# Selecting v over all rows of TensorE, and the last dilated queries in natural order

## The chip, the cores and the metric

The kernel runs on one core of one Trainium2 chip. The metric is the device time of one execution in microseconds (us), the median of several runs; lower is better. A core has five engines: TensorE (PE; its weight loads are shown apart as PEld), VectorE (DVE), ScalarE (ACT), GpSimd (POOL) and SyncE (SP). Matmuls write PSUM, which has eight banks; everything else lives in SBUF. Transfers run on 16 DMA engines. Here POOL issues the loads, which convert float32 to float16 on the way, and SP issues the stores.

## The reference

Attention over 8 batches, 8 heads, 576 positions and 64 features, with two kinds of window, followed by a soft mixture of 8 experts with 4 slots each:

```python
scores = scale * np.matmul(q, k.transpose(0, 1, 3, 2))
rel = pos[:, None] - pos[None, :]
mask_plain = (rel >= 0) & (rel < 32)
mask_dil = (rel >= 0) & (rel < 32 * 4) & (rel % 4 == 0)
masks = np.stack([mask_plain if h < 4 else mask_dil for h in range(8)])
x = softmax(np.where(masks, scores, -1e9)) @ v        # then (B*S, H*D) = (4608, 512)

logits = x @ phi                                      # phi: (512, 32)
d = softmax over the 4608 rows of logits
slot_input = d.T @ x                                  # 32 slots
slot_out[e] = relu(slot_input[e] @ w1[e]) @ w2[e]     # w1: (512, 1024), w2: (1024, 512)
c = softmax over the 32 columns of logits
out = c @ slot_out                                    # (4608, 512), float32
```

The softmax over all 4608 rows means that no expert can start before the last batch's attention is done, and that no row of the output can be written before the last expert.

## The kernel before

**Loads.** `load_batch` (L154) brings q, k and v of one batch into one of eight "home" tiles, with `DMA_DIRECT2D` issues on POOL. When a batch has been read out of its home, `load_w1` and `load_w2` (L236, L245) put an expert's weights there. POOL's order is written by hand (L599 puts POOL under a manual schedule): all eight batches, then w1 and w2 of experts 0 to 5, w1 of 6, w1 of 7, w2 of 6, and w2 of 7 in two halves. A load into a home waits for the home's last readers. The order of the other engines' instructions is the planner's, so the lines of one step may be spread between those of others.

**Attention** goes in 32 units of two heads of a batch, in the order plain, dilated, plain, dilated (L255). A unit's steps run staggered (L611 to L646): `transposes` of q and k, `scores`, `softmax_parts` (exponential on ACT, product with a mask on DVE), `values` (probabilities times v, with a column of ones in v that gives the denominators, then the division on DVE), and `x_transposes`. Per batch come `front_logits`, `front_rows` and `front_slots` for the logits, their exponentials by rows and the sum of slots. Queries and keys are taken in blocks of 128; the last block holds queries 512 to 575.

In the dilated units position 4t + c belongs to class c. Blocks 0 to 3 of the output are the first 128 queries of each class; block 4 has the last 16 of each class. Before, query t of class c stands in partition 32c + t of block 4, 16 used and 16 idle partitions a class. So block 4 takes 16 matmuls with 32 columns of weights each (L391 to L394: 4 classes, and two sources of v: rows of class c, and the last 64 positions), the copy into xT reorders it (L426), `front_rows` needs four extra narrow matmuls (`row_blocks`, L449), and the masks of the two parts are built once by `spread_masks` (L564).

**v for plain units and for the tails.** v arrives with four positions in one partition. `spread_v` (L193) copies the dilated one. `select_v` (L198) turns the plain one into blocks of 128 positions by matmuls with 0/1 matrices (`pick`): for each block, four matmuls over 32 partitions, which use 32 rows of TensorE at one of two row positions; two blocks go into one tile of the score banks (`ps_s`, tag "s") and ACT copies them out (L213). A third tile in the ring takes the last 64 positions: four matmuls over 16 partitions for the plain heads (L216), four with 32 columns for the dilated ones (L225), and one copy (L234).

**PSUM.** `ring` has two banks and serves, in turn, every transposed q, k and x, the logits, the rows, the sums of slots and the third tile of `select_v`; a new use waits until the one two before it has been copied out. `ps_s` has two tiles of two banks (scores; and two tiles of `select_v` a batch), `ps_o` two of one bank (values).

**The end.** `last_early`, `last_logits` and `last_slots` finish the last batch; `expert_in` and `expert_out` run the experts as the weights land, `sop` (L699) sums them, `so` is its copy (L716), and the output phase (L726 to L749) multiplies, scales on ACT and DVE, and stores on SP's queue.

Of the kernel before, what the change touches and what calls it, by code (L numbers as in the profile page):

```python
# [35 lines left out]
CL = S // DIL  # L36
DW = CL + 16
# [6 lines left out]
def constants():  # L44
    j = np.arange(128)[:, None]
    i = np.arange(QW)[None, :]
    d = i - j
    keep = ((d >= 0) & (d < WINDOW)).astype(np.float16)
    m, n = np.arange(128)[:, None], np.arange(64)[None, :]
    ends = (m // 32 == n // 16) & (m % 32 <= n % 16)  # L50
    band = np.concatenate([keep, ends], axis=1).astype(np.float16)
    ident = np.eye(128, dtype=np.float16)
    return band, ident
# [3 lines left out]
def kernel(  # L57
# [17 lines left out]
    mask = consts.tile([128, QW + 2 * N_SLOTS + 256], FP16, name="mask")  # L75
# [7 lines left out]
    nc.sync.dma_start(out=mask[:, 0 : QW + 64], in_=band_dram.ap())  # L83
# [14 lines left out]
    pick = kept([128, 4, 32, 4], "pick")  # L98
    stackI = kept([128, N_SLOTS], "stackI", FP32)
    upper = kept([128, 1], "upper", FP32)  # L100
    phi_by = kept([128, 4, 4, N_SLOTS], "phi_by")
# [10 lines left out]
    nc.vector.memset(phi_by, 0.0)  # L112
# [3 lines left out]
    P2 = kept([128, 2, 4, 2, 32], "P2")  # L116
# [4 lines left out]
    Er = [kept([128, 10, N_SLOTS], f"Er{i}") for i in range(2)]  # L121
# [6 lines left out]
    nc.vector.memset(P2, 0.0)  # L128
    nc.vector.memset(P2[0:1, :, :, 0, 16:32], 1.0)
# [68 lines left out]
    def select_v(b):  # L198
        raw, last = raws[b]["vp"], raws[b]["vt"]
        for i in range(2):  # L200
            sel = ps_s.tile([128, 2, 2, 4, D], FP32, name=f"sel{b}_{i}", tag="s")
            for r in range(4):
                for n in range(2):
                    rows = slice(64 * i + 32 * n, 64 * i + 32 * n + 32)
                    nc.tensor.matmul(  # L205
                        sel[:, n, 0],
                        pick[rows, r].rearrange("p i j -> p (i j)"),
                        raw[rows, :, r, :],
                        start=(r == 0),
                        stop=(r == 3),  # L210
                        tile_position=(64 * i + 32 * n, 0),
                    )
            nc.scalar.copy(out=vp[b % NV][:, 2 * i : 2 * i + 2, :, 0:D], in_=sel[:, :, 0])  # L213
        end = ring.tile([128, 2, 4, D], FP32, name=f"sel{b}_2", tag="ring")
        for r in range(4):
            nc.tensor.matmul(  # L216
                end[:, 0],
                pick[96:112, r].rearrange("p i j -> p (i j)"),
                last[:, 0:4, r, :],
# [3 lines left out]
            )  # L223
        for r in range(4):
            nc.tensor.matmul(  # L225
                end[32 * r : 32 * r + 32, 1],
                ident[96:112, 96:128],
                last[:, 4:8, r, :],
                start=True,
                stop=True,  # L230
                tile_position=(96, 32 * r),
                skip_group_check=True,
            )
# [66 lines left out]
    def scores(u):  # L300
# [3 lines left out]
        for part in range(2):  # L304
# [7 lines left out]
            for at, k0, q0, n in todo:  # L312
                for g in range(2):
                    ks = q0 - 32 * g - 64 * (at // DW) if k0 is None else k0
# [10 lines left out]
    def softmax_parts(u, tiles):  # L325
# [24 lines left out]
        if hp < 2:  # L350
# [8 lines left out]

        nc.vector.tensor_tensor(  # L360
            out=P2.rearrange("p a c s t -> p (a c) s t")[:, :, :, 0:16],
            in0=pr[:, :, :, 128:DW].rearrange("p a c (s t) -> p (a c) s t", s=2),
            in1=mask[:, QW + 64 :].rearrange("p (c s t) -> p c s t", c=8, s=2),
# [3 lines left out]
    def values(u):  # L367
# [7 lines left out]
        for half in range(2):  # L375
# [4 lines left out]
            for i, blk in enumerate(blocks):  # L380
                for h in range(2):
# [7 lines left out]
                    else:  # L389
                        for s in range(2):  # L390
                            for c in range(4):  # L391
                                vt = vp[b % NV][:, 5, hl + h] if s else vd[b % 2][:, 4 * (hl + h) + c]
                                mms.append((ot[32 * c : 32 * c + 32, i, h], P2[:, h, c, s], vt))
# [15 lines left out]
    def x_transposes(u):  # L409
# [11 lines left out]
        else:  # L421
# [4 lines left out]
            nc.vector.tensor_copy(  # L426
                out=xT[:, hp, 512:576].rearrange("c (t k) -> c t k", k=4),
                in_=rg[:, 512:640].rearrange("c (k t) -> c t k", k=4)[:, 0:16],
            )

# [19 lines left out]
    row_blocks = [(slice(0, 128), 128 * i, 1) for i in range(4)]  # L450
    row_blocks += [(slice(0, 128), c, 4) for c in range(4)] + [(slice(0, 128), 512, 1)]
    row_blocks += [(slice(32 * c, 32 * c + 32), 512 + c, 4) for c in range(4)]

    def rows(to, tokens, rhs, start, stop):
        for n, (part, at, step) in enumerate(row_blocks):
            w = step * (part.stop - part.start - 1) + 1
            nc.tensor.matmul(
                to[part, min(n, 9), :], tokens(at, at + w, step), rhs, start=start, stop=stop,
# [3 lines left out]
    def front_rows(b):  # L462
# [7 lines left out]
        ep = ring.tile([128, 11, N_SLOTS], FP32, name=f"e{b}", tag="ring")  # L470
        if b < B - 1:
            rows(ep, lambda a, z, s: ET[:, r0 + a : r0 + z : s], ident[:, 0:N_SLOTS], True, True)
            nc.vector.tensor_copy(out=Er[b % 2], in_=ep[:, 0:10])
        for n, (_, c0, nj) in enumerate(cols):
            nc.tensor.matmul(
                ep[:, 10, n : n + 1], ET[:, c0 : c0 + 127 * nj + 1 : nj], quarter, start=True, stop=True
            )
        if cols:
            n0 = cols[0][0]
            nc.vector.reciprocal(out=rrow[:, n0 : n0 + len(cols)], in_=ep[:, 10, 0 : len(cols)])  # L480

    def front_slots(b):
# [4 lines left out]
        for n, (g, blk, j) in enumerate(order):  # L487
            e_col = 8 + g if blk == 4 else 4 * g + blk
# [14 lines left out]
    def last_early(last):  # L503
# [4 lines left out]
        for dc in range(4):  # L508
# [8 lines left out]
        lr = last[:, 1, 0 : 11 * N_SLOTS].rearrange("p (i s) -> p i s", s=N_SLOTS)  # L517
        nc.tensor.matmul(
            lr[:, 8:10].rearrange("p i s -> p (i s)"), ident, mask[:, QW : QW + 64],
# [261 lines left out]
```

## Time and profile before

| | |
|---|---|
| three runs | 184.94, 185.99 and 186.16 us; median 185.99 |
| span of the profiled execution, first to last instruction | 183.5 us (the page has no other figure for it) |
| median of the runs less that span | 2.5 us |
| matmuls | 2595, with as many weight loads |
| loads by POOL's queue | 30.79 MB in SBUF; 93.9% of 16 engines' span |
| stores by SP's queue, with a few small loads | 9.89 MB; 13.4% |
| HBM read and written | 62.02 and 9.44 MB |
| select, L205 | 128 matmuls, 17.8 us busy, 307 ns from start to end of one |
| its two copies a batch, L213 | 16, 9.4 us busy, 590 ns |
| third tile: L216, L225, copy L234 | 5.6, 2.5 and 4.7 us busy |
| narrow values of L395 (32 columns) | 256 matmuls, 4.8 + 4.6 us busy |
| product for block 4, L360 | 16, 4.5 us busy, 282 ns |
| reorder of block 4, L426 | 16, 3.5 us busy, 221 ns |

Matmuls are pipelined: one takes 200 to 300 ns from start to end, while the next may start 30 to 110 ns after it. What PE pays is therefore read from the starts in the timeline, not from the mean length. The line of 40 slices shows busy tenths of equal parts of the span (9 is 90% or more). A chain of work is read downwards in order of time: start, length, and what ran or what was waited for; the step after a DMA is what that DMA released. In a row of waits come the waiting instruction, what released it, the sum in us, the number of waits and the longest.

### The profile page before, as it was taken

How to read it: one execution, taken by the hardware profiler on the slowest of the kernel's cores; microseconds unless marked ns; L12 is line 12 of the kernel's file. 1: busy time of each engine (PE TensorE's matmuls, PEld its weight loads, DVE VectorE, ACT ScalarE, POOL GpSimd, SP SyncE). 2: the span in 40 equal slices, each digit the busy share in tenths (PEclk: the TensorE clock that was granted, in tenths of full speed). 3: DMA queues.
4: the chain of work that ended last, by engine and by line, in shares of the span. 5: the costliest groups of instructions: out<-in, count | busy, mean ns of one | idle time of the engine just before them, and what ended most of it. 6: DMA issues, size and time to landing. Idle time of an engine off the chain costs nothing.

```text
span 183.5 us, 6054 instructions
## 1 busy us (share of the span) xinstructions
PE 151.8 (83%) x2595; PEld 105.8 (58%) x2595; DVE 117.1 (64%) x363; ACT 115.5 (63%) x208; POOL 46.9 (26%) x77
## 2 busy tenths in 40 slices
PE   1869999999988989998997998898979998885300
PEld 1637776677676667666765767666768644432000
DVE  7605886388877877878779687786970111496410
ACT  2248845689599789779878959977703022675410
POOL 7752555464554654401102001003100000000000
PEclk9999999999999999999999999999995589998555
DMA  5999999999999999999999999999999995199996
GB/s 103 183 203 203 202 203 201 202 202 204 204 201 201 204 199 204 226 211 221 212 216 216 212 216 216 218 212 218 218 214 220 212 208 105 75 440 427 427 427 262
DMA packets 23978, 41.06 MB, mean 224 GB/s; under 512 B 1680, under 2 KB 20240, under 8 KB 21136
## 3 DMA queue, kind: packets, MB, share of 16 engines
q0 software_dynamic: 21584, 30.79, 93.9%
q1 hardware_dynamic: 2368, 9.89, 13.4%
q8 instruction: 20, 0.33, 0.6%
q14 instruction: 6, 0.05, 0.1%
HBM read 62.02 MB, written 9.44 MB: 389 GB/s over the span
## 4 chain that ended last, share of the span: by engine, by line
DMA 74%; issue 15%; POOL 3%; ACT 2%; DVE 1%; PE 0%; POOLq 0%; DVEq 0%; SPq 0%
DMA home<-in_moe_w_dram 31%; DMA home<-in_v_dram 15%; DMA home<-in_k_dram 12%; DMA home<-in_q_dram 9%; DMA out_dram<-ot 7%; ACT ot L739 2%; DVE ot L741 1%; POOL home L250 1%; POOL home L162 1%; POOL home L239 1%; POOL home L184 0%; POOL home L187 0%; ACT so L716 0%; PE sop L699 0%; PE f L735 0%
## 5 line engine op out<-in xcount | busy, mean ns | idle before, releaser
L400 DVE TENSOR_TENSOR x<-o,rc 128x384 f16<-128x384 f32 x64 | 29.9, 482 | 0.5
L332 ACT ACTIVATE pr<-s 128x960 f16<-128x960 f32 (+1 forms) x32 | 24.7, 780 | 1.8 <-PE s L315 1.8
L344 ACT ACTIVATE pd<-s 128x640 f16<-128x640 f32 x32 | 20.9, 706 | 1.7 <-PE s L315 1.7
L162 POOL DMA_DIRECT2D home<-in_v_dram x24 | 16.6, 692 | 16.6 <-DMA home<-in_k_dram 11.6
L205 PE MATMUL sel<-home,pick 32*128 32x256 f16 x128 | 17.8, 307 | 1.4 <-DMA home<-in_v_dram 1.1
L399 DVE RECIPROCAL rc<-o 128x6 f32<-128x6 f32 x64 | 10.2, 177 | 13.5 <-PE o L395 13.4
L416 PE MATMUL rgx<-ident,x 128*128 128x128 f16 x160 | 15.6, 233 | 3.0 <-ACT qT L295 3.0
L741 DVE TENSOR_SCALAR ot<-f,rrow 128x512 f32<-128x512 f32 (+1 forms) x19 | 12.5, 716 | 7.7 <-DMA out_dram<-ot 5.2
L335 DVE TENSOR_TENSOR Pp<-pr,mask 128x960 f16<-128x960 f16 (+2 forms) x48 | 16.4, 394 | 0.4 <-ACT pr L332 0.4
L280 ACT COPY qT<-rgq 128x576 f16<-128x576 f16 x16 | 10.3, 641 | 9.0 <-PE rgq L275 8.5
L422 ACT COPY xT<-rgx 128x512 f16<-128x512 f16 x16 | 9.6, 601 | 10.0 <-PE rgx L416 10.0
L739 ACT ACTIVATE ot<-f,rrow 128x512 f32<-128x512 f32 (+1 forms) x19 | 11.2, 675 | 7.0 <-DMA out_dram<-ot 6.6
L239 POOL DMA_DIRECT2D home<-in_moe_w_dram x8 | 4.3, 534 | 44.4 <-PE rgq L290 36.5
L213 ACT CAST vp<-sel 128x512 f16<-128x512 f32 x16 | 9.4, 590 | 9.2 <-PE sel L205 9.0
L416 PEld LDWEIGHTS <-x 128*128 128x128 f16 x160 | 10.2, 102 | 7.2 <-issue 5.4
L735 PE MATMUL f<-so,ET 128*128 128x512 f16 (+1 forms) x38 | 11.0, 402 | 3.9 <-ACT ot L739 3.0
L275 PEld LDWEIGHTS <-home 96*64 96x64 f16 x384 | 11.9, 123 | 3.9 <-issue 2.0
L184 POOL DMA_DIRECT2D home<-in_k_dram x16 | 10.6, 661 | 10.1 <-DMA home<-in_q_dram 8.2
L395 PE MATMUL o<-vp,Pp 128*128 128x65 f16 x288 | 12.9, 203 | 0.0
L436 PE MATMUL l<-xT,phi 128*128 128x288 f16 x64 | 10.8, 304 | 2.0 <-ACT qT L280 1.7
L295 DVE COPY kTd<-rgk 128x576 f16<-128x576 f16 x16 | 12.0, 752 | 0.6 <-PE rgk L290 0.5
L295 ACT COPY qT<-rgq 128x576 f16<-128x576 f16 x16 | 10.3, 646 | 3.1 <-PE rgq L290 2.6
(105 smaller groups left out, 292.9 us busy)
## 6 DMA issues: line engine op xcount, KB each, us to landing
home<-in_moe_w_dram POOLq DMA_DIRECT2D x15, 1024.0 KB, 30.1
out_dram<-ot SPq DMA_DIRECT2D x7, 1024.0 KB, 7.5
home<-in_k_dram POOLq DMA_DIRECT2D x16, 288.0 KB, 9.9
home<-in_q_dram POOLq DMA_DIRECT2D x15, 288.0 KB, 9.7
home<-in_v_dram POOLq DMA_DIRECT2D x16, 256.0 KB, 9.8
out_dram<-ot SPq DMA_DIRECT2D x3, 512.0 KB, 6.5
home<-in_moe_w_dram POOLq DMA_DIRECT2D x2, 512.0 KB, 27.3
home<-in_v_dram POOLq DMA_DIRECT2D x8, 64.0 KB, 8.9
```

What stands on the lines that cost most here:

```text
L162: nc.gpsimd.dma_start(out=dst, in_=v[b, h0 : h0 + n_h, r0 : r0 + 4 * n_p, :].rearrange("h (p r) d -> p h (r d)", r=4),)
L205: nc.tensor.matmul(sel[:, n, 0], pick[rows, r].rearrange("p i j -> p (i j)"), raw[rows, :, r, :], start=(r == 0), stop=(r == 3), tile_posi ...
L275: nc.tensor.transpose(rg[64 * h : 64 * h + 64, r, :], raw[:, 2 * hp + h, D * r : D * r + D], ident[0:NP, 0:NP],)
L295: (nc.scalar.copy if nm == "q" else nc.vector.tensor_copy)(out=dst[:, 0:S].rearrange("c (g p a) -> c g p a", g=4, a=3), in_=rg.rearrange(" ...
L332: nc.scalar.activation(out=pr, in_=st[:, :, 0:n], func=AF.Exp, scale=SCALE)
L335: nc.vector.tensor_tensor(out=Pp[:, :, b0 : b0 + nb, 0:w], in0=pr[:, :, at : at + nb * w].rearrange("p h (t c) -> p h t c", c=w), in1=mask ...
L344: nc.scalar.activation(out=pr[:, part].rearrange("p c e t -> p e c t"), in_=st[:, :, 0 : 2 * DW].rearrange("p e (c t) -> p e c t", c=2), f ...
L395: nc.tensor.matmul(to, lhs, rhs, start=(n == 0), stop=(n == len(mms) - 1), skip_group_check=True)
L400: nc.vector.tensor_tensor(out=x[:, blocks[0] : blocks[0] + nb, D * hl : D * hl + 2 * D].rearrange("p t (h d) -> p t h d", h=2), in0=ot[:, ...
L416: nc.tensor.transpose(rg[:, 128 * blk : 128 * blk + 128], x[:, blk, hl : hl + 128], ident)
L739: nc.scalar.activation(out=ot[:, j, d0:d1], in_=fp, func=AF.Copy, scale=scale)
L741: nc.vector.tensor_scalar(out=ot[:, j, d0:d1], in0=fp, scalar1=scale, scalar2=None, op0=ALU.mult)
```

## The change

- `select_v`: for each block of 128 positions four matmuls now run over all 128 partitions, with `pick` as a zero-padded matrix from which a shifted window of 128 columns is cut. Its two tiles are in the ring, not in the score banks. The third tile takes all eight heads at once: four matmuls of 512 columns over 16 partitions with a second matrix, `pick_end`.
- Block 4 of the dilated units is kept in natural order: query 4t + c in partition 4t + c. Its probabilities go into `Pm` (four matmuls a head with 128 columns of weights, one per class) and `Pt` (one matmul a head for the last 64 positions): 10 matmuls a unit in place of 16. The product on DVE becomes two.
- `front_rows` and the rows of the last batch have 9 matmuls in place of 13; `Er` has 9 blocks, not 10. The copy of block 4 into xT no longer reorders, and takes 64 columns as they stand.
- Setup: `spread_masks` goes, `spread_ends` builds `pick_end`, the mask of the tails comes from the constant `band` (same size), `shut` is a small tile of its own, and `spread_phi` casts phi once and uses 16 matmuls of 32 columns in place of 4 of 128.

No transfer is added, moved or resized, and POOL's order is the same. Core of the diff:

```diff
-    P2 = kept([128, 2, 4, 2, 32], "P2")
+    Pm = kept([128, 2, 4 * 129], "Pm")
+    Pt = kept([128, 2, 128], "Pt")
...
     def select_v(b):
         raw, last = raws[b]["vp"], raws[b]["vt"]
         for i in range(2):
-            sel = ps_s.tile([128, 2, 2, 4, D], FP32, name=f"sel{b}_{i}", tag="s")
-            for r in range(4):
-                for n in range(2):
-                    rows = slice(64 * i + 32 * n, 64 * i + 32 * n + 32)
+            sel = ring.tile([128, 2, 4, D], FP32, name=f"sel{b}_{i}", tag="ring")
+            for n in range(2):
+                for r in range(4):
                     nc.tensor.matmul(
-                        sel[:, n, 0],
-                        pick[rows, r].rearrange("p i j -> p (i j)"),
-                        raw[rows, :, r, :],
+                        sel[:, n],
+                        pick[:, 2 * i + n, 3 - r : 131 - r],
+                        raw[:, :, r, :],
                         start=(r == 0),
                         stop=(r == 3),
-                        tile_position=(64 * i + 32 * n, 0),
                     )
-            nc.scalar.copy(out=vp[b % NV][:, 2 * i : 2 * i + 2, :, 0:D], in_=sel[:, :, 0])
-        end = ring.tile([128, 2, 4, D], FP32, name=f"sel{b}_2", tag="ring")
+            nc.scalar.copy(out=vp[b % NV][:, 2 * i : 2 * i + 2, :, 0:D], in_=sel)
+        end = ring.tile([128, 2, 4, D], FP32, name=f"end{b}", tag="ring")
         for r in range(4):
             nc.tensor.matmul(
-                end[:, 0],
-                pick[96:112, r].rearrange("p i j -> p (i j)"),
-                last[:, 0:4, r, :],
+                end.rearrange("p a h d -> p (a h) d"),
+                pick_end[96:112, 128 * r : 128 * r + 128],
+                last[:, :, r, :],
                 start=(r == 0),
                 stop=(r == 3),
                 tile_position=(96, 0),
-            )
-        for r in range(4):
-            nc.tensor.matmul(
-                end[32 * r : 32 * r + 32, 1],
-                ident[96:112, 96:128],
-                last[:, 4:8, r, :],
...
+        tails = pr[:, :, :, 128:DW].rearrange("p a c (s t) -> p a c s t", s=2)
         nc.vector.tensor_tensor(
-            out=P2.rearrange("p a c s t -> p (a c) s t")[:, :, :, 0:16],
-            in0=pr[:, :, :, 128:DW].rearrange("p a c (s t) -> p (a c) s t", s=2),
-            in1=mask[:, QW + 64 :].rearrange("p (c s t) -> p c s t", c=8, s=2),
+            out=Pm.rearrange("p a (c x) -> p (a c) x", c=4)[:, :, 0 : 4 * TAIL : 4],
+            in0=tails[:, :, :, 0].rearrange("p a c t -> p (a c) t"),
+            in1=mask[:, None, 128:CL].broadcast_to([128, 8, TAIL]),
+            op=ALU.mult,
+        )
+        nc.vector.tensor_tensor(
+            out=Pt[:, :, 0 : 4 * TAIL].rearrange("p a (t c) -> p a c t", c=4),
+            in0=tails[:, :, :, 1],
+            in1=ends[:, None].broadcast_to([128, 2, 4, TAIL]),
             op=ALU.mult,
         )
...
-                        for s in range(2):
-                            for c in range(4):
-                                vt = vp[b % NV][:, 5, hl + h] if s else vd[b % 2][:, 4 * (hl + h) + c]
-                                mms.append((ot[32 * c : 32 * c + 32, i, h], P2[:, h, c, s], vt))
+                        for c in range(4):
+                            mms.append((ot[:, i, h], Pm[:, h, 128 * c : 128 * c + 128], vd[b % 2][:, 4 * (hl + h) + c]))
+                        mms.append((ot[:, i, h], Pt[:, h], vp[b % NV][:, 5, hl + h]))
...
-            nc.vector.tensor_copy(
-                out=xT[:, hp, 512:576].rearrange("c (t k) -> c t k", k=4),
-                in_=rg[:, 512:640].rearrange("c (k t) -> c t k", k=4)[:, 0:16],
-            )
-
+            nc.vector.tensor_copy(out=xT[:, hp, 512:576], in_=rg[:, 512:576])
...
-    row_blocks = [(slice(0, 128), 128 * i, 1) for i in range(4)]
-    row_blocks += [(slice(0, 128), c, 4) for c in range(4)] + [(slice(0, 128), 512, 1)]
-    row_blocks += [(slice(32 * c, 32 * c + 32), 512 + c, 4) for c in range(4)]
+    row_blocks = [(128 * i, 1) for i in range(4)] + [(c, 4) for c in range(4)] + [(512, 1)]
...
-        for r in range(4):
-            nc.tensor.matmul(
-                pp,
-                pick[:, r].rearrange("p i j -> p (i j)"),
-                phi_by[:, :, r, :],
+            for r in range(4):
+                nc.tensor.matmul(
+                    pp[:, kc], pick[:, kc, 3 - r : 131 - r], phi_h[:, r, :],
```

## The prediction

> **What bounds the kernel now.** I read the page first: queues and the row of 40 slices, then the chain, then the seam where the weights end, and only then PE, where the change is.
>
> ```profile
> span 183.5 us, 6054 instructions
> PE 151.8 (83%) x2595; PEld 105.8 (58%) x2595; DVE 117.1 (64%) x363; ACT 115.5 (63%) x208; POOL 46.9 (26%) x77
> DMA  5999999999999999999999999999999995199996
> q0 software_dynamic: 21584, 30.79, 93.9%
> q8 instruction: 20, 0.33, 0.6%
> ```
>
> PE is the busiest compute engine, but the DMA engines are full in every slice except the first and two near the end: 30.79 MB of loads on POOL's queue, then the stores. The chain in order of time says who released whom at that gap:
>
> ```profile
> 128.48 28.27 DMA home<-in_moe_w_dram
> 156.74 0.04 issue
> 156.78 0.42 PE sop L699 x4
> 157.21 0.02 issue
> 157.23 0.59 ACT so L716
> ```
>
> The last half of w2 of expert 7 is issued at 128.48 and lands at 156.74; four sop matmuls, the copy and the output phase follow. POOL was held before that issue: its waits have "home L239 <- PE rgq L290" with 36.5 us in 3 waits (home 7 must be read out), the last ending at 126.91. That is no starvation: behind that point only w1 of 7, w2 of 6 and w2 of 7 were issued, 3 MB, 14.6 us at the 215 GB/s of these windows, yet the last landed 29.8 us later. So 15 us of loads were still queued, and PE could be 15 us later or any amount earlier without moving the landing. The seam itself, by windows (columns: PE, PEld, DVE, ACT, POOL busy, clock, DMA share, GB/s):
>
> ```profile
> 156.20:156.40 0.20, 0.20 (x11) 0.13 (x4) 0.00 (x0) 0.00 (x0) 0.00 (x0) 1.00 0.01 0
> 156.60:156.80 0.20, 0.14 (x8) 0.01 (x3) 0.00 (x0) 0.00 (x0) 0.00 (x0) 1.00 0.00 0
> ```
>
> PE is busy right up to the seam and idle only some 0.06 us there. Groups of four sop follow each other 0.22 us apart (23 of them take 1.72 us from 155.47), and the group ahead of the last starts at about 156.35, so without the wait the last would start at 156.57 instead of 156.78. **PE's own chain ends only 0.2 us before the loads**: a PE that is faster gains nothing, a PE that is more than 0.2 us slower is seen in full. The question is therefore the sign of PE's change.
>
> **What the change does, part by part.** PE pieces of one batch, from the timeline (start, length):
>
> ```profile
> 76.36 0.28 PE L205 MATMUL sel<-home,pick 32*128 32x256 f16 x1
> 76.57 0.29 PE L475 MATMUL e<-quarter,ET 128*128 128x1 f16 x4
> 79.44 0.39 PE L205 MATMUL sel<-home,pick 32*128 32x256 f16 x4
> 79.69 0.59 PE L216 MATMUL sel<-home,pick 16*128 16x256 f16 x4
> 80.21 0.29 PE L225 MATMUL sel<-home,ident 16*32 16x256 f16 x4
> 80.44 0.24 PE L315 MATMUL s<-qT,kTd 64*128 64x144 f16 x2
> ```
>
> - Pace: L216 is 4 matmuls of 256 columns in 0.59, the last 0.27 long, so 0.107 each. L205 has 4 in 0.39: two pairs, the two row groups side by side. But each piece pays at its edges: one L205 alone holds PE 0.21 (76.36 to 76.57) for 0.107 of work, and 0.08 to 0.1 more goes before it (the transposes ahead run 0.056 apart, the step into the select is 0.15). The planner cuts the 16 L205 of this batch into seven pieces.
> - Select, removed: the pieces hold PE 0.32+0.21+0.34+0.21+0.30+0.21+1.00 = 2.59 us of this batch (start to the next other start, L216 and L225 included), with seven entries of 0.08 3.2 us. Added: 16 full-array matmuls of 256 columns, 16 x 0.107 = 1.7, with no change of form against the 128-row transposes beside them; 4 of 512 columns at 0.216 (L735: 5 in 1.24, one 0.377) = 0.86; one entry and exit, 0.2: 2.8. Net -0.4; at worst all edges stay (+0.2), at best the old pieces cost more elsewhere (-0.7). I take -0.4, the row's own account.
> - The Trainium skill, TensorE: Matmul & The Clock Gate, Part 3, says that K = 32 matmuls in distinct row groups run side by side, which speaks against filling the array: by that alone the select goes from 8 x 0.107 = 0.86 to 1.7, +0.9 a batch. The trace agrees on the pairs (4 in 0.39). The Trainium skill, TensorEngine Tiling (Array Packing), Key Properties, says that a change of tiling mode drains the engine; the 0.21 steps agree, and with it the select is the -0.4 above.
> - Dilated values: 16 narrow matmuls per unit start in four-abreast groups, 0.34 us with both edges (75.32 to 75.65); 10 full ones at 0.031 (18 in 0.72) are 0.31. Zero, +-0.1.
> - Rows: 13 become 9 a batch, the four 32-column ones and their edges go: -0.15. In the tail 52 become 36 at 0.04 (52 in 2.20): -0.6 once. spread_phi: 4 become 16, 12 x 0.04 = +0.5 once.
> - Sum on PE: about -0.5 a batch, -4 us by the end of attention (bounds +1 to -8). It lands on PE's wait for weights. If that cover were gone it would be 4 us of gain.
> - DVE, startup: memsets +0.6 (Pm 0.5, pick_end 0.3, Pt 0.17, shut 0.16, less P2 and phi_by 0.27 each, by the rows of like size), mask building -1.1 + 0.3, phi casts -0.9. Cover: the cast of q0 ends at 4.44 and the first transposes start at 7.42 behind PE's warm matmuls; 2.4 us to spare.
> - DVE, steady: the 282 ns product becomes two with a stepped output, 0.2 each at a guess between 219 (128 elements) and 282: +0.1 a dilated unit; the copy L426 (221) shrinks a little. DVE is 64% busy; only one PE wait in the run is on it (0.9 us). Without that cover +1.9 us over 16 units.
> - SP and POOL: band has the same 56 KB, no DMA moves, POOL waits for the same readers of home. Nothing there.
> - Loads: about 160 fewer matmuls and as many weight loads; at 64 bytes (0.33 MB over 5190 instructions) one of the 20 instruction blocks goes, 0.9 us (0.6% of 16 engines' span over 20) on one of 16 rings. The Trainium skill, Runtime: NRT & Kernel Launch, Instruction fetch mechanics, has such blocks at 16 KiB; the q8 line agrees (0.33 MB over 20). The landing moves only if that ring is the last: bounds -0.9 to +0.9 (blocks fall on other rings), taken -0.1.
>
> Sum: 183.5 - 0.1 = 183.4 of span. The page gives no second figure for this execution; the median of the three runs is 185.99, 2.5 over the span, and I carry that: **185.9 us**.
>
> **Rivals.**
> 1. *The ring becomes the wait, slower.* Two selects a batch move from the score banks to the ring, whose uses go from 17 to 19 a batch on two banks. PE already waits for it:
>
> ```profile
> PE rgx L416 <- ACT qT L295: 3.0, 6, 0.5
> PE l L436 <- ACT qT L280: 1.7, 5, 0.6
> ```
>
> Each select holds a bank for 0.86 of filling, 0.2 to the release and 0.59 of copy (L213): 1.65, 3.3 a batch. Filling, release and copy of the other uses come to some 22 us a batch (8 transposes at 1.3, 4 of x and 2 logits at 1.1, rows 1.9, slots 1.2, end 1.5), of 30 in two banks (batch 14.8 us): 73% goes to 84%. What queues behind a waiting select on PE is the next unit's scores, and ACT's exponential waits for those. Against it: the second select (0.86) covers most of the first one's copy (0.8), the score banks get free, and ACT stands idle 0.75 and 0.96 in this stretch. For it: a copy behind a 0.97 or 1.31 us exponential makes PE wait that long. It decides where the waits pass 0.55 a batch; at 1.0 a batch over 7 batches PE ends 7 - 4 - 0.2 = 3 us late: 189.
> 2. *Packing was worth more than its edges, slower.* If the 0.2 us steps are waits that any select would meet, only the pairs (4 in 0.39) and the four-abreast values count: +0.9 select, +0.1 end, +0.2 values, 1.2 a batch, 7 batches 8.4, less 0.2: 194. It decides from 0.03 a batch on. The steps stand at every change of form and at no other place, which speaks against it. This is the case that Part 3 of the page named above describes.
> 3. *PE's clock, slower.* The same 18 matmuls take 1.17 us early and 0.72 later:
>
> ```profile
> 35.80 1.17 PE L395 MATMUL o<-vp,Pp 128*128 128x65 f16 x18
> ...
> 42.95 0.72 PE L395 MATMUL o<-vp,Pp 128*128 128x65 f16 x18
> ```
>
> PE runs slow until about 39 us, though the page writes 9 for the clock there. A batch then takes about 18 us instead of 14.8. If the other mix keeps it slow for two batches more, 6.5 - 4 - 0.2: 188. Full-array work with fewer gaps speaks rather for an earlier rise, which would be hidden.
> 4. *The loads end sooner, faster.* The last loads trail off: 16 rings end between about 152 and 156.7 (from 152 on the windows fall from 209 to 131, 111, 98, 29 GB/s). With evener rings the landing comes up to 2.6 us sooner (about 154.1): 183.4. Nothing in the change aims at that but the one block.
>
> **How the numbers follow.** Loads hold the end: 0.76, 185.9 with its own range 184.9 to 187.0 (blocks +-0.9, scatter of the runs 184.9 to 186.2). Ring 0.11, packing 0.04, clock 0.03, loads sooner 0.06. Within 1% (about what a measurement of this kernel can tell from no change; 1.9 us) is the first case but for some 0.02: 0.74. Slower 0.19: the three rivals and a hundredth of the first. Faster 0.07: the fourth and a hundredth. The range reaches to the ring's nearer half and part of the fourth: 184.3 to 188.5, which leaves out about 0.05 below and 0.1 above.
>
> **What would show it.** Right: the last weights land at 156.7 +-0.9 and release the last four sop; PE idles for microseconds before that instead of 0.06; select matmuls start 0.107 apart with no 0.2 steps around them; unit 31 ends some 4 us sooner. Ring: waits of sel, end or rgq on ACT vp over 4 us in all, and no DMA at the seam. Packing: the batch period over 14.8. Clock: the 1.1 us form of the 18 matmuls after 45 us. I am wrong about the floor if the landing itself moves by over 1 us.

## The result and the profile after

The changed kernel takes 198.3 us (four runs, 197.52 to 199.79); the kernel before took 185.76 us in the runs beside them (184.94 to 186.16). The ratio is 1.068, with an interval of 1.063 to 1.074: slower by 12.5 us. The prediction said 185.9, from 184.3 to 188.5. Some executions of a kernel run some per cent longer than its others; the ratios here and below leave them out (one of b_ring's four, 205.47 us, and two of b_spread's four, 193.04 and 193.53, the first of them the profiled one). The execution of the changed kernel that was profiled took 198.24 us. Its page, in the lines that were shown of before:

```profile
span 196.4 us, 5748 instructions
PE 157.8 (80%) x2435; PEld 109.6 (56%) x2435; DVE 120.4 (61%) x375; ACT 114.9 (58%) x208; POOL 47.1 (24%) x77
DMA  5999999999999999999999999999599900099997
q0 software_dynamic: 21584, 30.79, 88.3%
q8 instruction: 19, 0.31, 0.6%
```

There are 160 matmuls fewer and one instruction block fewer, as the prediction had it. But the DMA line now has a 5 in slice 29, where the loads ran out of issues for a moment, and three slices of 0, in which the loads were all but over and PE still worked on the experts. The chain in order of time, at its end:

```profile
141.63 16.02 DMA home<-in_moe_w_dram
157.65 3.15 PE h L653 x25
...
166.14 0.94 PE h L653 x16
167.16 0.61 ACT hs L661
168.23 1.43 PE sop L677 x23
170.62 3.09 ACT ot L717 x6
```

Before, the last weights released four sop matmuls at 156.78 us. Now all 23 sop of the end run in one piece at 168.23, behind PE's own experts. The first line must not be read as a wait for the loads: it ties a DMA to the first h matmuls, which read experts 0 and 1, loaded long before. The view of the tile siT of the same kernel lists two candidates, one by the weight loads and one by the matmuls, for what is one idle stretch of 0.7 us:

```profile
  DVE siT L632: 0.7, 1
  DMA home<-in_moe_w_dram: 0.7, 1
```

siT starts at 157.31 and takes 0.29; h starts 0.35 us after siT's start. In b_ring, a kernel told of below whose loads end at another time, the distance is the same and siT is named:

```profile
156.04 0.29 DVE L657 TENSOR_TENSOR siT<-last,rtot 128x128 f16<-128x128 f32 x1
156.39 3.17 PE L678 MATMUL h<-home,siT 128*32 128x512 f16 x25 [0.65 <-DVE siT L657]
```

So the end is PE's, and it came late out of attention. The experts start at 157.65 us, against 145.03 before (+12.6), and take 12 us in both. The first exponential of a batch on ACT marks where the 12.6 arose. First after, then before, from the timeline:

```profile
44.52 1.41 ACT L327 ACTIVATE pr<-s 128x960 f16<-128x960 f32 x2
...
78.57 1.41 ACT L327 ACTIVATE pr<-s 128x960 f16<-128x960 f32 x2
...
95.67 1.41 ACT L327 ACTIVATE pr<-s 128x960 f16<-128x960 f32 x2
...
130.13 1.40 ACT L327 ACTIVATE pr<-s 128x960 f16<-128x960 f32 x2
```

```profile
44.56 1.50 ACT L332 ACTIVATE pr<-s 128x960 f16<-128x960 f32 x2
...
74.22 1.50 ACT L332 ACTIVATE pr<-s 128x960 f16<-128x960 f32 x2
...
89.07 1.50 ACT L332 ACTIVATE pr<-s 128x960 f16<-128x960 f32 x2
...
119.05 1.50 ACT L332 ACTIVATE pr<-s 128x960 f16<-128x960 f32 x2
```

Both stand at 44.5 us at the same place. From there five batches take 85.6 us after and 74.5 before, 11.1 more; the last batch and the tail take 27.5 against 26.0, 1.5 more. Together that is the 12.6. A batch in steady state takes **17.10 us (78.57 to 95.67) where it took 14.85** (74.22 to 89.07): 2.25 more. The prediction had 0.5 less. This batch period is the measure of most experiments below.

One stretch of a batch of after, from the timeline (start, length, engine, line, and in brackets the idle time before it with its releaser):

```profile
101.26 0.44 PE L417 MATMUL rgx<-ident,x 128*128 128x128 f16 x5 [0.63 <-ACT kTp L275]
...
101.54 1.04 PE L211 MATMUL sel<-home,pick 128*128 128x256 f16 x8
...
102.51 0.24 PE L310 MATMUL s<-qT,kTp 64*128 64x160 f16 x1
102.61 0.59 ACT L218 CAST vp<-sel 128x512 f16<-128x512 f32 x1 [1.40 <-PE sel L211]
...
102.68 1.05 PE L211 MATMUL sel<-home,pick 128*128 128x256 f16 x8
...
103.66 1.03 PE L221 MATMUL end<-home,pick_end 16*128 16x512 f16 x4
103.76 0.59 ACT L218 CAST vp<-sel 128x512 f16<-128x512 f32 x1 [0.56 <-PE sel L211]
...
104.73 0.59 ACT L229 CAST vp<-end 128x512 f16<-128x512 f32 x1 [0.38 <-PE end L221]
...
105.14 0.20 DVE L400 RECIPROCAL rc<-o 128x6 f32<-128x6 f32 x1 [1.91 <-PE o L396]
```

PE does the whole select in two pieces, 0.97 and 1.94 us, with a single score matmul between them; ahead of them stand the x transposes of one unit, behind them values and the queries of the next. ACT and DVE stand idle beside it (1.40 + 0.56 + 0.38, and 1.91 us). Before, the select came in seven pieces with the units' work between them.

One of these seven shows what the pieces were good for. First before, between the sums of slots (tile u) and the x transposes; then the same place in after:

```profile
78.41 0.51 PE L489 MATMUL u<-x,Er 128*32 128x256 f16 x10
78.85 0.28 PE L205 MATMUL sel<-home,pick 32*128 32x256 f16 x1
79.06 0.45 PE L416 MATMUL rgx<-ident,x 128*128 128x128 f16 x5
```

```profile
83.03 0.51 PE L483 MATMUL u<-x,Er 128*32 128x256 f16 x10 [0.23 <-ACT qT L275]
84.17 0.44 PE L417 MATMUL rgx<-ident,x 128*128 128x128 f16 x5 [0.63 <-ACT kTp L275]
```

Both u and rgx take turns in the ring, so rgx waits until ACT has copied the transposed keys out of the bank that it gets. From u to rgx it is 0.65 us before, with a piece of select in between, and 1.14 us after, of which PE is idle for 0.63.

### The profile page after: what moved, and what is told of

The parts are those of the page before. It is cut to its first block, busy times and chain, and to the rows that moved or that the text cites. A ratio compares the mean times of both kernels' runs of the same rounds, so it can differ in the third digit from the quotient of the medians.

```text
span 196.4 us, 5748 instructions
## 1 busy us (share of the span) xinstructions
PE 157.8 (80%) x2435; PEld 109.6 (56%) x2435; DVE 120.4 (61%) x375; ACT 114.9 (58%) x208; POOL 47.1 (24%) x77
## 4 chain that ended last, share of the span: by engine, by line
DMA 29%; issue 25%; PE 20%; DVE 11%; ACT 6%; POOL 4%; POOLq 0%; ACTq 0%; DVEq 0%; SPq 0%
DMA home<-in_moe_w_dram 19%; DMA out_dram<-ot 6%; DMA home<-in_v_dram 4%; PE sel L211 4%; PE h L653 3%; DVE x L401 2%; PE o L396 2%; PE end L221 2%; DVE kTd L290 2%; PE s L310 2%; PE rgx L417 2%; ACT ot L717 2%; DVE P L348 2%; PE sop L677 1%; ACT pd L339 1%
## 5 line engine op out<-in xcount | busy, mean ns | idle before, releaser
L327 ACT ACTIVATE pr<-s 128x960 f16<-128x960 f32 (+1 forms) x32 | 23.7, 766 | 0.1
L339 ACT ACTIVATE pd<-s 128x640 f16<-128x640 f32 x32 | 22.4, 711 | 0.9 <-PE s L310 0.7
L417 PE MATMUL rgx<-ident,x 128*128 128x128 f16 x160 | 14.5, 221 | 6.9 <-ACT kTp L275 3.8
L330 DVE TENSOR_TENSOR Pp<-pr,mask 128x960 f16<-128x960 f16 (+2 forms) x48 | 17.1, 389 | 4.4 <-ACT pr L327 4.4
L218 ACT CAST vp<-sel 128x512 f16<-128x512 f32 x16 | 9.4, 589 | 17.2 <-PE sel L211 17.2
L211 PE MATMUL sel<-home,pick 128*128 128x256 f16 x128 | 18.4, 291 | 0.2 <-DVE kTd L290 0.2
L719 DVE TENSOR_SCALAR ot<-f,rrow 128x512 f32<-128x512 f32 (+1 forms) x19 | 12.5, 717 | 7.7 <-DMA out_dram<-ot 5.4
L310 PE MATMUL s<-qT,kTd 64*128 64x144 f16 (+1 forms) x256 | 15.2, 199 | 0.5 <-ACT pr L327 0.4
L275 ACT COPY qT<-rgq 128x576 f16<-128x576 f16 x16 | 10.2, 638 | 8.8 <-PE rgq L270 8.8
L211 PEld LDWEIGHTS <-pick 128*128 128x128 f16 x128 | 12.3, 104 | 3.1 <-issue 0.8
L396 PE MATMUL o<-vp,Pp 128*128 128x65 f16 x288 | 13.8, 196 | 0.1
L421 DVE COPY xT<-rgx 128x576 f16<-128x576 f16 x16 | 7.2, 452 | 10.7 <-PE rgx L417 10.7
L396 PEld LDWEIGHTS <-Pp 128*128 128x128 f16 x288 | 11.3, 98 | 3.6 <-issue 2.5
```

The lines of the kernel that those rows point to most:

```text
L211: nc.tensor.matmul(sel[:, n], pick[:, 2 * i + n, 3 - r : 131 - r], raw[:, :, r, :], start=(r == 0), stop=(r == 3),)
L310: nc.tensor.matmul(st[:, g, at : at + n], kT[64 * g : 64 * g + 64, ks : ks + 128], qT[64 * g : 64 * g + 64, q0 : q0 + n], start=True, stop ...
L327: nc.scalar.activation(out=pr, in_=st[:, :, 0:n], func=AF.Exp, scale=SCALE)
L330: nc.vector.tensor_tensor(out=Pp[:, :, b0 : b0 + nb, 0:w], in0=pr[:, :, at : at + nb * w].rearrange("p h (t c) -> p h t c", c=w), in1=mask ...
L339: nc.scalar.activation(out=pr[:, part].rearrange("p c e t -> p e c t"), in_=st[:, :, 0 : 2 * DW].rearrange("p e (c t) -> p e c t", c=2), f ...
L396: nc.tensor.matmul(to, lhs, rhs, start=(n == 0), stop=(n == len(mms) - 1), skip_group_check=True)
```

## The experiments

Two sorts of kernel: the changed one with a part undone, and the kernel before with a part of the change alone. "Score banks" is where `select_v` had its two tiles before. In the diffs, minus is the kernel named as the base.

**a_score**: the changed kernel with the two tiles back in the score banks, all else as changed.

```diff
-            sel = ring.tile([128, 2, 4, D], FP32, name=f"sel{b}_{i}", tag="ring")
+            sel = ps_s.tile([128, 2, 4, D], FP32, name=f"sel{b}_{i}", tag="s")
```

> The changed kernel with its two full-row select tiles back in the score banks; all else as changed. Ring theory (the select tiles hold the two ring banks and stop the transposes): back to 186 to 188 us. Rows theory (128-row selects cost more than packed ones): stays at 197 to 199. Block-4 theory (the two stepped DVE products, 0.45 and 0.50 us in the trace where the one before took 0.28, delay the copies behind them): stays at 196 to 198.

Measured: 185.22 us, ratio to before 0.996 (0.994 to 0.998); period 15.54. One line takes back all of the 12.5 us and 1.56 of the 2.25 a batch. Of the kernels that were run several times it is the fastest, by 0.4% against before.

**a_packed**: as a_score, and the select of the four blocks again over 32 rows a matmul, in pairs, as before the change.

```diff
-                        pick[:, 2 * i + n, 3 - r : 131 - r],
-                        raw[:, :, r, :],
+                        packp[rows, r].rearrange("p i j -> p (i j)"),
+                        raw[rows, :, r, :],
...
+                        tile_position=(64 * i + 32 * n, 0),
```

> The changed kernel with the select of blocks 0 to 3 as it was (32 rows, score banks); block 4, its masks and the third tile as changed. Ring theory and rows theory: 186 to 188. Block-4 theory: 196 to 198.

Measured: 185.67 us, ratio 1.000 (0.996 to 1.003); period 15.47. Full rows against packed rows is 0.07 us a batch, although by the starts in the timeline the packed select holds PE 0.59 us less (2.36 against 2.95).

**b_score**: the kernel before, with only the 128-row matmuls, in the score banks.

```diff
-                        pick[rows, r].rearrange("p i j -> p (i j)"),
-                        raw[rows, :, r, :],
+                        pickf[:, 2 * i + n, 3 - r : 131 - r],
+                        raw[:, :, r, :],
```

> The kernel before with only the select of blocks 0 to 3 over 128 rows, in the score banks. Ring theory: 186. Rows theory: 196. Block-4 theory: 186 to 188.

Measured: 185.92 us, ratio 1.000 (0.997 to 1.003); period 14.95, 0.10 over before.

**b_ring**: b_score with the two tiles in the ring.

```diff
-            sel = ps_s.tile([128, 2, 4, D], FP32, name=f"sel{b}_{i}", tag="s")
+            sel = ring.tile([128, 2, 4, D], FP32, name=f"sel{b}_{i}", tag="ring")
```

> The kernel before with only the select of blocks 0 to 3 over 128 rows and in the ring; block 4 and the third tile as before. Ring theory and rows theory: 196 to 198. Block-4 theory: 186 to 188.

Measured: 197.98 us (median of all four), ratio 1.062 (1.058 to 1.066); period 16.67, 1.72 over b_score. Rows and block 4 fall as the main cause: the ring alone, in the kernel before, makes nearly the whole loss. The waits of PE hardly show it: those of rgx on copies come to 6.3 us in the run here and 3.5 in b_score, for 12 us of time. Waits of ACT and DVE (total, times, longest), first of b_score, then of b_ring:

```profile
DVE rc L399 <- PE o L395: 9.8, 13, 1.6
```

```profile
ACT vp L213 <- PE sel L206: 21.4, 16, 3.0
DVE rc L399 <- PE o L395: 21.4, 15, 3.8
```

DVE waits for values 11.6 us longer in the run. The list of groups has ACT's wait for the select at 7.7 us in b_score, 21.4 here.

**b_vals**: b_score with the two tiles in the two banks of the values.

```diff
-            sel = ps_s.tile([128, 2, 4, D], FP32, name=f"sel{b}_{i}", tag="s")
+            sel = ps_o.tile([128, 2, 4, D], FP32, name=f"sel{b}_{i}", tag="o")
```

> The kernel before with 128-row selects of blocks 0 to 3 in the values' banks (two of one bank, 8 uses a batch become 10), so the same serial chain of two tiles and copies, but not in front of the transposes. Block theory: the planner can put other work between, period 14.9 to 15.4, time 185 to 187. Any pool of two single banks is as bad: period 16.4 to 17, time 196 to 199.

Measured: 184.99 us (one run); period 15.37. A pool of two banks of one tile each is not what costs: in that of the values the same tiles cost 0.42 a batch over b_score.

**b_spread**: b_ring, but the three tiles are asked for one in each of three units instead of one behind the other.

```diff
-            select_v(u // 4 + 1)
+            select_v(u // 4 + 1, (2,))
+        if u % 4 in (1, 2) and u // 4 + 1 < B:
+            select_v(u // 4 + 1, (u % 4 - 1,))
```

> The kernel before with 128-row selects in the ring (as in b_ring, batch period 16.67 us), but its three ring tiles of a batch are asked for in three different units (4b+1, 4b+2, 4b+3) and not in one. Block theory (three selects in a row in the ring put 3 us of TensorE work in one piece between a unit's transposes, while ACT and DVE run dry): batch period 14.9 to 15.4, time 185 to 187. Bank-time theory (the ring's two banks are full, 19 uses a batch are too many wherever they stand): period 16.4 to 17, time 196 to 199.

Measured: 188.59 and 190.08 us, ratio 1.020 (1.012 to 1.027), so slower than before, by 1 to 3%; period 15.45 to 16.04, 15.7 in the mean of four, at a granted clock of 1.00. As many turns of the ring, and 1.0 of the 1.72 gone: neither theory whole.

**b_ring_thin**: b_ring with one of the four matmuls of each block, which leaves out three quarters of v; the turns of the ring stay, the fill is a quarter.

```diff
-                for r in range(4):
+                for r in range(1):
```

> b_ring with one matmul in place of four in each select of blocks 0 to 3, so that three quarters of v are left out; the ring's turns and copies are the same, the fill is a quarter. Block theory: period 15.0 to 15.4 (1.3 us of the 1.7 goes), time 186 to 188. Turns theory (each further turn of the ring costs a wait for a copy, whatever its fill): period 16.2 to 16.7, time 195 to 198.

Measured: 201.6 us (one run), but not for the ring's sake. Two of its batches ran 15.79 and 15.78, the two between them 19.84 and 18.55, and there the granted clock was at half (columns: length, busy us of PE, PEld, DVE, ACT and POOL, clock, DMA share, GB/s):

```profile
82.60:96.30 13.70, 13.19 (x152) 9.10 (x152) 6.32 (x19) 7.70 (x16) 1.06 (x2) 0.50 1.03 215
96.30:103.10 6.80, 5.63 (x134) 4.44 (x131) 6.29 (x19) 5.14 (x9) 0.00 (x0) 1.00 1.02 214
103.10:113.40 10.30, 10.00 (x117) 6.90 (x117) 5.08 (x17) 5.73 (x11) 1.06 (x2) 0.50 1.04 216
```

At full clock 0.9 of the 1.72 goes with the fill and 0.8 stays. The time itself says nothing on the ring, and the split holds only as far as a select this short is placed as the long one was.

**a_score_flat**: a_score with the two products for block 4 written without a step, so that block 4's probabilities stand in other columns than they should.

```diff
-            out=Pm.rearrange("p a (c x) -> p (a c) x", c=4)[:, :, 0 : 4 * TAIL : 4],
+            out=Pm.rearrange("p a (c x) -> p (a c) x", c=4)[:, :, 0:TAIL],
...
-            out=Pt[:, :, 0 : 4 * TAIL].rearrange("p a (t c) -> p a c t", c=4),
+            out=Pt[:, :, 0 : 4 * TAIL].rearrange("p a (c t) -> p a c t", c=4),
```

> a_score (batch period 15.54 us against 14.95 in b_score) with the two products of block 4 written without steps, so that block 4's probabilities stand in wrong columns. Product theory (stepped 16-bit writes make them 0.45 and 0.50 us): the products take about 0.2 each, the period falls to 14.9 to 15.1. TensorE theory (10 full values and the 512-column third tile): the period stays at 15.4 to 15.6. The time is 184 to 187 in both, since the loads end at 156 to 157.

Measured: 185.74 us (one run); period 14.92, 0.62 under a_score. The groups of both (busy, mean ns), first a_score:

```profile
L362 DVE TENSOR_TENSOR Pt<-pd,mask 128x128 f16<-128x128 f16 x16 | 8.2, 511 | 0.0
L356 DVE TENSOR_TENSOR Pm<-pd,mask 128x128 f16<-128x128 f16 x16 | 7.3, 455 | 0.0
```

```profile
L356 DVE TENSOR_TENSOR Pm<-pd,mask 128x128 f16<-128x128 f16 x16 | 3.7, 229 | 0.0
L362 DVE TENSOR_TENSOR Pt<-pd,mask 128x128 f16<-128x128 f16 x16 | 3.5, 219 | 0.0
```

The same elements cost twice as much when they are written with a step of four, 0.52 us more a dilated unit, 1.04 a batch. The batch gets 0.62 shorter without the step; the planner's order of PE moved along with it (the select in eight pieces, six in a_score), so the split between the two is not shown. The Trainium skill, VectorE: DVE Perf Modes, Mode 2×_1P, asks for a step of one where 16-bit elements are to go two at a time; these rows agree in direction.

**b_ring_early**: b_ring with all three tiles asked for two units earlier, still one behind the other.

```diff
+        if u % 4 == 1 and u // 4 + 1 < B:
+            select_v(u // 4 + 1)
...
-            select_v(u // 4 + 1)
```

> b_ring (batch period 16.67 us) with all three selects of a batch asked for in unit 4b+1 and not 4b+3, so in one piece but in another place. Block theory: one piece is as bad there, period 16.3 to 17.3. Place theory (only the spot between the transposes of units 4b+2 and 4b+4 hurts): period 14.9 to 15.6. The time follows: 195 to 200, or 185 to 188.

Measured: 188.43 us (one run; before took 187.01 beside it); period 15.55. Its select, from the timeline:

```profile
73.11 1.92 PE L206 MATMUL sel<-home,pickf 128*128 128x256 f16 x16
74.19 0.59 ACT L213 CAST vp<-sel 128x512 f16<-128x512 f32 x1 [0.64 <-PE sel L206]
...
75.07 0.59 ACT L213 CAST vp<-sel 128x512 f16<-128x512 f32 x1 [0.29 <-PE sel L206]
```

The block is at least as solid as in b_ring and in the same two banks, and 1.12 of the 1.72 is gone. So most of it is neither the number of turns nor that they come together, but where in the batch they stand. The other 0.60 stays open.

**b_ring_scores**: b_ring with the select asked for one step later, behind the scores of a unit.

```diff
+        if u % 4 == 0 and 0 < u < NU:
+            select_v(u // 4)
...
-            select_v(u // 4 + 1)
```

> b_ring (batch period 16.67 us) with its select asked for one loop step later, right after the scores of unit 4b+5 and ahead of the values that need it; it keeps its ring turns between x of unit 4b+2 and the next transposes. Scores theory (the select stands ahead of the next unit's scores in TensorE's order, so ACT has no exponential to do meanwhile): period 14.9 to 15.6, waits of ACT on TensorE for the select under 1.2 us a batch. Turn theory (what hurts is the ring's turns between these transposes, whoever stands ahead): period 16.2 to 17. Time 185 to 188, or 194 to 198.

Measured: 201.78 us (one run); period 16.66 to 16.67 at full clock, with two batches at 18.06 and 20.66 beside stretches of half clock of 3.4 and 10.2 us. The planner put the scores back where they were: the ring's turns and PE's order came out as in b_ring (eight selects, one score matmul, eight selects and the third tile). So this run repeats b_ring's period and does not decide between the two theories.

**b_ring3 and c_ring3**: b_ring, and the kernel before, with three banks in the ring (values one bank, and the output phase's pool two, to make room).

```diff
-        tc.tile_pool(name="ring", bufs=2, space=bass.MemoryType.PSUM)
+        tc.tile_pool(name="ring", bufs=3, space=bass.MemoryType.PSUM)
...
-    ps_o = tc.alloc_tile_pool(name="ps_o", bufs=2, space=bass.MemoryType.PSUM)
+    ps_o = tc.alloc_tile_pool(name="ps_o", bufs=1, space=bass.MemoryType.PSUM)
```

> b_ring with three banks in the ring and one in place of two for the values (and two buffers in place of three for the output tiles). If the ring's two banks are what the select exhausts, the period falls from 16.67 to within 0.4 of the same kernel without the ring's selects (c_ring3, the other run of this pair). If it is the piece of 3 us in TensorE's order, the distance to c_ring3 stays at 1.2 to 1.8.

> The kernel before with three banks in the ring, one for the values and two buffers for the output tiles: what the banks' move does without the select's. Two theories agree: period 14.5 to 16.5, by how often the one bank of the values is waited for; it is the base that b_ring3 is read against.

Measured: b_ring3 186.49 us, period 15.17; c_ring3 186.55 us, period 13.98 (one run each, before 187.01). A third bank takes 1.50 a batch off b_ring, and 0.87 off the kernel before, so the ring's own share of b_ring's loss shrinks; the two still differ by 1.19. By the expectation that is just the second case, a piece of 3 us in PE's order, and not two banks that run out. But most of the 1.19 is the select itself: by the starts it holds PE 1.62 us a batch in c_ring3 and 2.60 in b_ring3. It is all in one piece in b_ring3, and but for two matmuls in c_ring3. First c_ring3, then b_ring3:

```profile
63.99 0.63 PE L205 MATMUL sel<-home,pick 32*128 32x256 f16 x14
```

```profile
76.22 1.91 PE L206 MATMUL sel<-home,pickf 128*128 128x256 f16 x16
```

Fourteen packed matmuls in 0.63 us, sixteen full ones in 1.91: with the pieces together, packing saves PE about 1 us a batch, and 0.07 where the planner cuts them up (a_packed against a_score). How much of the 1 us reaches the period is not shown, since the select of c_ring3 is also in the score banks and that of b_ring3 in the ring. The Trainium skill, TensorE: Matmul & The Clock Gate, Part 3, has such matmuls run side by side; the first row agrees, and the kernel before, cut into seven pieces, got little of that gain.

c_ring3 also tests the floor. Its batches are 0.87 us shorter than before's and its time is the same, because the loads hold the end. Its chain:

```profile
124.29 32.58 DMA home<-in_moe_w_dram
156.91 0.64 PE sop L699 x4
```

with PE idle for 2.08 us ahead of the last line, waiting for that DMA.

## Why the prediction was wrong, point by point

- **The floor: right.** Last weights land at 156.7 us before, 156.9 in c_ring3. Periods from 13.98 to 15.54 (c_ring3, a_score_flat, before, b_score, b_ring3, b_vals, a_packed, a_score) all end between 185.0 and 186.6 us. A faster PE gains nothing. a_score is the slowest of them: its 23 sop of the end run unbroken from 155.90, so the loads no longer stop it. b_ring_early, whose period is the same but whose experts start 2.0 us later (147.51 against 145.48), ends at 188.4. "More than 0.2 us slower is seen in full" held too: PE left attention 12.6 us late, and the median rose by 12.5. One detail was wrong: that PE could be 15 us later without moving the landing. In b_ring POOL's last wait ended at 138.36, 11.4 us later than before, and the loads still ended as before (no traffic from 156 to 157). In after it ended at 140.07, 13.2 us later, and the loads end at 159.0, some 2 us later than the 156.7 of before; a landing that moves by over 1 us was the prediction's own sign against the floor. It did not set the end, for the sop that read the last weights start at 168.23 or later. The windows of after:

```profile
158.50:159.00 0.50, 0.50 (x12) 0.24 (x8) 0.00 (x0) 0.00 (x0) 0.00 (x0) 0.50 0.15 33
159.00:159.50 0.50, 0.50 (x12) 0.22 (x8) 0.00 (x0) 0.00 (x0) 0.00 (x0) 0.50 0.00 0
```

- **The step that failed: "Sum on PE: about -0.5 a batch".** It added up how long each piece holds PE and took the order of the pieces as given, as if PE's time were the sum of its pieces. Measured +2.25, in three parts: the ring 1.56 (17.10 less a_score's 15.54), the stepped products 0.62 (15.54 less 14.92), everything else 0.07 (14.92 less 14.85). The timelines show where the time lies. Below is PE's time in one batch, each matmul counted from its start to the start of the next one, in us:

| matmuls of | before | a_score_flat | a_score | after | b_score | b_ring |
|---|---|---|---|---|---|---|
| q and k transposes | 2.60 | 2.60 | 2.56 | 3.36 | 2.60 | 3.37 |
| sums of slots (u) | 0.44 | 0.44 | 0.44 | 1.14 | 0.44 | 1.14 |
| values (o) | 2.53 | 2.64 | 3.06 | 3.12 | 2.52 | 2.67 |
| select with the third tile | 2.59 | 3.20 | 2.95 | 2.91 | 3.00 | 2.72 |
| all others | 6.70 | 6.03 | 6.53 | 6.57 | 6.38 | 6.78 |

  From a_score to after, 1.50 of the 1.56 falls on the q and k transposes and on u, which take turns in the ring; from b_score to b_ring it is 1.47 of the 1.72. The select itself does not get longer. The rows of u and rgx above show how: a wait for a copy, which other work filled before, stands open, and the select takes its own time elsewhere on top. That the transposes of q and k lose their time in the same way is argued, not shown.
- **Select, -0.4: small, and of the other sign.** From its first start to the next other start the select holds PE 2.59 us a batch before, 3.00 in b_score, 2.95 in a_score, 2.91 after. Edges go, but the packed pairs go with them. By the period full rows cost 0.10 (b_score) and against packed rows in the changed kernel 0.07.
- **Values, rows, tail: about right together.** They lie in the 0.07; by the table the values hold PE 0.11 us longer in a_score_flat than before, within the 0.1 or so that was allowed. Rows and tail were not measured alone.
- **DVE, "two products 0.2 each at a guess": wrong by more than two.** 453 and 508 ns, from the rows of after. The guess lay between two rows of other products, and neither of those writes with a step. The cover, a DVE at 64%, was an average, and "only one PE wait in the run is on it (0.9 us)" was read too narrowly: the same view has five more, of 0.8 us in all, of rgq on the copy kTd. Of 1.04 us a batch 0.62 came through with the order that the planner then chose; the values, which read the two products, hold PE 0.42 us a batch longer in a_score than in a_score_flat.
- **SP and POOL, "nothing there": the issues are the same, but their times are not.** POOL's last wait ended later with PE (140.07 against 126.91), and the loads ran dry once. That did not set the end.
- **Rival 1, the ring: the right culprit, at 0.11, by another mechanism.** Its price was put at 1.0 a batch and the point of decision at 0.55; it measured 1.56 in the changed kernel and 1.72 in the kernel before. The argument against it was that the second select covers the first one's copy and that the banks are 84% full, so that waits should be short. That much held: there is no row of PE waiting on the copies vp at all. What the count of banks could not see is order: with turns in the ring, the select's three tiles come nearly in one block of 2.9 us, ahead of the next unit's queries and keys, which take the next turns, and no longer as pieces between the other users of the ring. ACT and DVE run dry beside it. So the sign that the prediction named, "waits of sel, end or rgq on ACT vp over 4 us", did not appear; no DMA at the seam, its second half, did. ACT's wait for the select rose, to 17.2 us after from 9.0 before (the rows of its groups). The sign named for packing, a period over 14.8, appeared too, and would have led to the wrong rival.
- **Rival 2, packing: falls as the cause** (0.07 to 0.10). The 1.19 between b_ring3 and c_ring3 is close to its price of 1.2 a batch by chance: the price counted the values too, and these kernels differ in the banks of the select as well.
- **Rival 3, the clock: the other way.** After the clock rose by 24.6 us at the latest, before at 39.0. This hid some of the loss: with slow batches before and fast ones after, both stand at 44.5 us.

Shown: the ring is the cause of the time (a_score, b_ring); place decides more than count (b_ring_early, b_spread); the lost time stands at the q and k transposes and at u (the table); a third bank takes 1.50 a batch away, of which 0.87 also comes to the kernel before. Only argued: that the select's pieces, spread as before, are what would fill these waits. b_ring3 speaks for care here: its q and k transposes hold PE 3.2 us, nearly as long as b_ring's, and its DVE waits for values 20.7 us against b_ring's 21.4, at a period 1.5 us shorter; there the scores hold PE less (2.8 against 3.5). Not tried: a bank for the select alone, since all eight are in use.

## What to carry to other kernels

A tile that moves into a shared ring of PSUM banks takes a place in an order of turns; ask what stands behind it in that order, and what waits its work has been filling until now, not only how full the banks are. The time that a piece holds an engine is no gain when the engine would wait in its place. A price per instruction holds only for the same access pattern: a product with a stepped output needs a row of a stepped product. Before giving a faster engine any worth, find what ends last; here a period anywhere from 13.98 to 15.54 us gave the same time.

## What the runs showed of the hardware

- **The clock changes on a grid.** In b_ring the granted clock fell to half at 47.6 and again at 98.8 us, each time for 3.4 us; 51.2 us apart, 15 times 3.41. Each of the six drops between 45 and 110 us in b_ring, b_ring_scores and b_ring_thin follows a stretch in which PE was busy about three quarters of the time (2.54 to 2.64 of 3.41 us). In each pair of windows below the first is the stretch ahead and the second the drop (columns as in the windows above). b_ring:

```profile
95.40:98.80 3.40, 2.64 (x59) 2.00 (x59) 3.02 (x11) 2.89 (x5) 0.00 (x0) 1.00 1.04 217
98.80:102.20 3.40, 3.28 (x17) 1.95 (x17) 1.81 (x5) 0.56 (x2) 0.00 (x0) 0.50 1.03 217
```

  b_ring_scores:

```profile
96.20:99.60 3.40, 2.64 (x59) 2.01 (x59) 3.01 (x12) 2.77 (x5) 0.00 (x0) 0.99 1.03 214
99.60:109.80 10.20, 9.95 (x82) 6.42 (x83) 3.87 (x10) 3.95 (x8) 1.06 (x2) 0.50 1.03 216
```

  The Trainium skill, TensorE: Matmul & The Clock Gate, HAM oscillation, gives "no PE-idle gaps" over about 3.4 us as the rule. The two drops shown came with 0.76 us of idle time in all in the stretch ahead. Busy time does not decide it either: windows with 2.54 of 3.41 and 35 to 42 matmuls in after, one with 2.42 in before, and one with 2.45 and 62 matmuls in b_ring_thin itself had no drop behind them. What counts as activity stays open. A drop made its batch 1.3 to 4.1 us longer.
- **The first rise depends on the work.** Before needs 39.0 us and c_ring3 40.7, with PE busy 31.5 of the 34 us up to 39; with 128-row selects the rise was complete at 14 to 26 us in most kernels (33.2 in b_spread, 41.7 in b_ring_thin; a_score rose at 15.3 and had one drop, from 35.8 to 39.2), and a_packed, without them, rose at 27.2. What in the work decides it stays open.
